# Attention and gated feed-forward on one core: the second batch's attention moved from the prologue into chunk 0's first layer

## The chip, the cores and the metric

The kernel runs on one core of a Trainium2 chip. A core has five engines with a queue of instructions each: TensorE (PE, matrix products), VectorE (DVE), ScalarE (ACT), GpSimd (POOL) and SyncE (SP, which here only issues transfers). Every queue is worked off in order; where an instruction needs another engine's result, it waits on a semaphore, and everything behind it in its queue waits too. The metric is the device time of one execution in microseconds (us); lower is better. The median of three runs before the change is 1016.38 us.

## What is computed

```python
# q, k, v: (8, 8, 576, 64) float32     w_gate, w_val: (512, 1536) float64     w_out: (1536, 512) float64
kv  = einsum('bhsd,bhse->bhde', k, v)          # one 64 x 64 matrix per batch and head
out = einsum('bhsd,bhde->bhse', q, kv)
x   = out / sqrt(mean(out * out, -1) + 1e-6) * g_norm
x   = x.transpose(0, 2, 1, 3).reshape(4608, 512)
y   = (sigmoid(x @ w_gate) * (x @ w_val)) @ w_out
```

The weights arrive as 64-bit floating point numbers, and the kernel turns them into float32 itself.

## The kernel before

**Tiling.** The 4608 tokens are nine chunks of 512. A batch has 576 tokens, so chunk 0 lies wholly in batch 0, and chunk 1 holds the last 64 tokens of batch 0 and the first 448 of batch 1. The hidden width 1536 is twelve blocks of 128. Chunk 0 goes through the feed-forward plainly: the first layer is twelve blocks of 8 matmuls of 128x512 (`Plain.mm`, L561: four over the contraction for the gate, four for the value), the second layer 48 matmuls (`second`, L808). Chunks 1 to 8 use a scheme with fewer products in each layer (26 sets of products, L932 and L1036), for which sums of blocks of weights (`w1_sums`, L741, on GpSimd), of x (`x_sums`, L830, on VectorE) and of hidden values (L722, mostly on GpSimd) are formed beforehand.

**Weights.** `convert(u)` turns one unit, 128x1024 numbers, from float64 into float32 in five VectorE steps and two ScalarE steps: `s0` takes the high bits of the mantissa (L179) and `s1` the exponent (L190); `a0` (L184) and `a1` (L195) are ScalarE's conversions of these two; `s2` (L200) adds the low word, `s3` (L204) the sign, `s4` (L211, L213) multiplies mantissa and exponent word. The exponent words lie in `cz`, a tile with two buffers in SBUF. There are 18 units: 0 to 11 serve the twelve first-layer blocks in their order, 12 to 17 the second layer, two blocks of rows each. A unit's 1 MB comes through `load_unit`, into three staging buffers.

**Attention, in two forms.** Batches 0 and 1 are handled early, by pairs of heads, eight pairs in all (`NE = 2 * NHP`). For a pair `attention(n)` has k-v products (KV, L276), their copy (KVO), the turn of q by TensorE (Q, L287) and its copy (QO), the product with q (U, L306), its square (SQ, ScalarE), sums (SUM, VectorE), root (ROOT, ScalarE), the norm (NORM, VectorE: reciprocal and one product), the turn of x (X, L333) and its copies (XO). Batches 2 to 7 are handled later in the other form, `feed(b)`: `load_late` brings k and v into `h_more`, `kv_mm` does all four pairs' k-v products at once (L366, L372), twelve ScalarE copies put them into `kvq` (L377), VectorE turns q in blocks of 32 (`turn`, L383), and `two_pairs` does U for two pairs (L407, 72 small matmuls into the tile `at` in PSUM, of which there is one), square, two sums, root, two norm operations on VectorE (L425) and the turns of x (L432), whose result 16 transfers on SP put into place. These steps stand at numbered places between the products of the chunk before.

**Order.** The prologue is written out by hand in `order`, a string of tokens: the steps above with the pair's number, `c0.1` and `a0.1` for conversion steps of a unit, `b0.1.2` for matmul 2 of the value half of first-layer block 0, `w2` for loading unit 2, and `warmN` for N matmuls without use. It interleaves eight pairs with blocks 0 to 3 of chunk 0 and units 0 to 4. As the root and the sigmoid need different tables of ScalarE, the first two blocks' results are copied out (CG, CV) and get their sigmoid (S) and product (M) once all eight pairs are through. From block 4 on `plain` runs: beside the first six matmuls of a block one conversion step each is placed, and the gate and the product of the block before at matmuls 0 and 2. Batch 2's `kv_mm` stands after block 8, its copies after block 9, the weight sums `w1_sums(0)` after block 10.

**Stores.** Rows of batches 0 and 1 leave the kernel in up to 96-row pieces, those of later batches in 32-row pieces, because the two forms of attention order tokens differently inside a batch (`store`, L503).

## Time and profile before

| | us |
|---|---|
| median of three runs (1016.28 to 1017.71) | 1016.38 |
| the profiled execution | 1015.84 |
| its span, first to last instruction | 1014.1 |
| TensorE busy | 1006.5 (99%) |
| VectorE busy | 727.1 (72%) |
| GpSimd busy | 598.9 (59%) |
| ScalarE busy | 350.2 (35%) |

The granted TensorE clock is full in the whole span. Between 100 and 160 us VectorE is busy for 8 to 10 of every 10 us and GpSimd for nearly all of them; between 160 and 260 us GpSimd is busy for 93 us. From 360 us on TensorE is busy without a break.

In the lines of the timeline the columns are: start (us from the span's start), length (us, of the whole merged group), engine, line, operation, output and inputs, shape, count, and in brackets the idle time before it and what ended it. An fp32 matmul has two records. Instructions overlap at their ends, so the distance from start to start is what one costs in a full queue.

### The profile page before, as it was taken

What the parts mean: (1) busy time and instruction counts of PE and PEld (TensorE: products, weight loads), DVE (VectorE), ACT (ScalarE), POOL (GpSimd) and SP (SyncE); (2) the same over time, 40 slices, a digit from 0 to 9 for tenths busy, and PEclk for the clock granted to TensorE, in tenths of its full rate; (3) what the DMA queues carried; (4) which work ended last, traced back from release to release, by engine and by line L of the source; (5) the groups of instructions that cost most, each with busy time, mean ns of one, the idle gap of its engine ahead of it and who ended that gap; (6) DMA issues with size and microseconds to landing.
All of it is one profiled execution on the core that took longest, in us unless ns stands there. A gap on an engine that the chain in (4) does not pass through costs nothing.

```text
span 1014.1 us, 18347 instructions
## 1 busy us (share of the span) xinstructions
PE 1006.5 (99%) x6914; PEld 828.0 (82%) x6914; DVE 727.1 (72%) x1211; ACT 350.2 (35%) x609; POOL 598.9 (59%) x965
## 2 busy tenths in 40 slices
PE   9999999999999999999999999999999999999998
PEld 8644447888888888888888888888888888888887
DVE  4899899899668846775678666866688556755672
ACT  4654422442154304441254115421453033213320
POOL 0001999998448642967177706962496439744963
PEclk9999999999999999999999999999999999999999
DMA  9975314644778468646765577556764546444514
GB/s 264 278 237 191 125 42 157 220 143 163 235 245 301 165 194 262 225 159 200 232 234 194 150 229 248 195 160 190 235 214 153 178 155 208 161 156 158 211 59 124
DMA packets 101128, 193.89 MB, mean 191 GB/s; under 512 B 27408, under 2 KB 74128, under 8 KB 101040
## 3 DMA queue, kind: packets, MB, share of 16 engines
q0 software_dynamic: 20976, 112.87, 32.9%
q1 hardware_dynamic: 72896, 77.75, 25.2%
q10 hardware_dynamic: 7168, 2.10, 0.9%
q8 instruction: 55, 0.90, 0.4%
q14 instruction: 33, 0.27, 0.1%
HBM read 160.04 MB, written 25.56 MB: 183 GB/s over the span
## 4 chain that ended last, share of the span: by engine, by line
PE 74%; POOL 2%; issue 0%; DVE 0%; POOLq 0%
PE mm L932 47%; PE mm L1036 24%; PE at L407 2%; PE at L366 1%; POOL h L722 1%; POOL w_ring L1007 0%; POOL h_more L722 0%; PE at L372 0%; POOL w L770 0%; DVE sg L902 0%; POOL w L1007 0%; POOLq L1007 0%
## 5 line engine op out<-in xcount | busy, mean ns | idle before, releaser
L932 PE MATMUL mm<-xs,w 128*128 128x256 f32 x1428 | 332.0, 380 | 0.0
L932 PEld LDWEIGHTS mm<-xs,w 128*128 128x128 f32 x1428 | 270.4, 190 | 37.4 <-DVE temps L902 0.3
L932 PE MATMUL mm<-xT,w 128*128 128x256 f32 x948 | 230.0, 380 | 0.0
L932 PEld LDWEIGHTS mm<-xT,w 128*128 128x128 f32 x948 | 179.4, 190 | 25.5 <-issue 1.0
L902 DVE TENSOR_TENSOR sg<-sg,mm 128x512 f32<-128x512 f32 (+1 forms) x176 | 100.8, 599 | 93.1 <-PE mm L932 45.7
L770 POOL DMA_DIRECT2D w<-kept x84 | 46.9, 558 | 190.7 <-PE mm L932 188.4
L1036 PE MATMUL mm<-w,h 128*128 128x256 f32 x630 | 143.4, 379 | 0.9 <-POOL h L894 0.5
L1036 PEld LDWEIGHTS mm<-w,h 128*128 128x128 f32 x630 | 119.5, 190 | 17.9 <-POOL h L894 0.9
L898 ACT COPY temps<-mm 128x512 f32<-128x512 f32 (+1 forms) x128 | 66.0, 537 | 190.0 <-PE mm L932 94.9
L894 POOL TENSOR_TENSOR h<-h,sg 128x512 f32<-128x512 f32 x72 | 97.6, 1372 | 50.3 <-DVE h L902 33.2
L722 POOL TENSOR_TENSOR h<-h 128x128 f32<-128x128 f32 x216 | 113.4, 537 | 16.5 <-DVE h_more L722 13.1
L1036 PE MATMUL mm<-w,h_more 128*128 128x256 f32 x474 | 108.2, 379 | 0.0
L891 ACT ACTIVATE sg<-sg 128x512 f32<-128x512 f32 x96 | 59.7, 630 | 131.4 <-DVE sg L902 131.4
L1036 PEld LDWEIGHTS mm<-w,h_more 128*128 128x128 f32 x474 | 90.1, 190 | 12.2
L898 ACT COPY sg<-mm 128x512 f32<-128x512 f32 (+1 forms) x112 | 57.1, 510 | 91.2 <-PE mm L1036 48.8
L722 POOL TENSOR_TENSOR h_more<-h 128x128 f32<-128x128 f32 x120 | 58.5, 490 | 33.9 <-DVE h L894 29.6
L561 PE MATMUL mm<-xT,w 128*128 128x512 f32 x176 | 77.7, 594 | 0.0
L902 DVE TENSOR_TENSOR temps<-temps,mm 128x512 f32<-128x512 f32 (+1 forms) x96 | 59.2, 617 | 25.5 <-PE mm L1036 17.2
L902 DVE TENSOR_TENSOR temps<-mm,temps 128x512 f32<-128x512 f32 (+1 forms) x64 | 39.8, 621 | 50.6 <-PE mm L1036 23.6
L898 ACT COPY h<-mm 128x512 f32<-128x512 f32 x48 | 28.1, 585 | 125.5 <-PE mm L932 110.5
L902 DVE TENSOR_TENSOR sg<-mm,sg 128x512 f32<-128x512 f32 (+1 forms) x64 | 39.6, 618 | 43.7 <-PE mm L932 21.9
L741 POOL TENSOR_TENSOR h_more<-w 128x256 f32<-128x256 f32 x10 | 12.8, 1299 | 97.4 <-PE at L366 97.4
(132 smaller groups left out, 1324.5 us busy)
## 6 DMA issues: line engine op xcount, KB each, us to landing
w<-kept POOLq DMA_DIRECT2D x42, 896.0 KB, 5.0
w<-kept POOLq DMA_DIRECT2D x90, 384.0 KB, 4.6
w<-kept POOLq DMA_DIRECT2D x42, 768.0 KB, 5.4
q<-in_q_dram SPq DMA_DIRECT2D x24, 288.0 KB, 3.0
out_dram<-sg SPq DMA_DIRECT2D x104, 64.0 KB, 1.7
st<-in_moe_w_gate_dram SPq DMA_DIRECT2D x12, 512.0 KB, 5.5
st<-in_moe_w_val_dram SPq DMA_DIRECT2D x12, 512.0 KB, 6.6
h_more<-in_k_dram SPq DMA_DIRECT2D x24, 256.0 KB, 5.0
```

The lines of the kernel that those rows point to most:

```text
L366: nc.tensor.matmul(ps[HD * e:HD * e + HD, n // 2, n % 2], mains[n, "k"][:, c], mains[n, "v"][:, c], start=(n % 2 == 0 and j == 0), stop=Fa ...
L407: nc.tensor.matmul(u[HD * e:HD * e + HD, r, o:o + HD], qTs[QB * r:QB * r + QB, (n0 + which) % 2, c:c + PH], kvq[QB * r:QB * r + QB, (n0 + ...
L561: nc.tensor.matmul(self.ps[i], w[("wg", "wv")[i], self.f][:, m, :], xT[self.c][:, m, :], start=(m == 0), stop=(m == NMT - 1), skip_group_c ...
L722: ops.append((eng, lambda v=v, x=x, sign=sign, y=y, eng=eng: eng.tensor_tensor(out=h_form(v, j), in0=h_form(x, j), in1=h_form(y, j), op=op ...
L741: nc.gpsimd.tensor_tensor(out=w1_slot(j, w_at[v]), in0=w1_slot(j, w_at[x]), in1=w1_slot(j, w_at[y]), op=op_of(sign))
L770: nc.gpsimd.dma_start(out=granule(g)[:, 0:n], in_=kept1[g // NPA % N3, g % NPA][:, 0:n])
L891: nc.scalar.activation(out=o["o" + step[1]], in_=o["o" + step[1]], func=AF.Sigmoid)
L894: mult.tensor_tensor(out=o[x], in0=o[x], in1=o[y], op=ALU.mult)
L898: nc.scalar.copy(out=o[out_], in_=o[expr])
L902: tt(out=o[out_], in0=o[x], in1=o[y], op=ALU.add if sign == "+" else ALU.subtract)
L932: nc.tensor.matmul(regions[name][1][:, g], ws[:, g], xf[c][wv], start=(new and g == 0), stop=True, skip_group_check=True)
L1036: nc.tensor.matmul(regions[name][1], h_form(hv, j), ws[:, j], start=(used[i] and j == 0), stop=(j == N3 - 1), skip_group_check=True)
```

## The change

Only batch 0's four pairs stay early (`NE = NHP`). The hand-written order ends with block 0 of chunk 0 and unit 1; CG, CV, S and M are gone, and the first block's sigmoid is read from PSUM as for the others. Blocks 1 to 11 go through `plain`, whose steps now come from a written table: place p is matmul p of these 88, and the names are `CV` (the next conversion step), `LL` and `LL2` (loads of k and v of batches 1 and 2), `KV`, `C0` to `C3` and `KV2`, `D0` to `D3` (k-v products and copies for the two batches), `Q0` to `Q3` (q loads), `t10` (turn of pair 1, half 0), `W0` (`w1_sums(0)`), and `a..`, `b..` for the steps of the two groups of two pairs. Batch 1 so takes the form of `feed`, with three differences: its q goes into parts of the hidden tiles `h_main`, which are not in use yet, its four rest loads are issued by SP, not by ScalarE, and its norm is 18 ScalarE activations with a scale for each partition. The exponent words of units 15, 16 and 17 lie in the tile `at` in PSUM. Rows of batch 1 are stored in 32-row pieces. From chunk 1 on the order of work is as before.

```diff
-    NE = 2 * NHP
+    NE = NHP
...
+            if b == 1:
+                i = n - NE
+                t = h_main[2 - i // 2].rearrange("p s c -> p (s c)")[0:NP, (i % 2) * 2 * NJ * HD:(i % 2 + 1) * 2 * NJ * HD]
+                t = t.rearrange("p (h c) -> p h c", h=2)
...
-                nc.scalar.dma_start(out=rest[...], in_=src[...])
+                (nc.sync if b == 1 else nc.scalar).dma_start(out=rest[...], in_=src[...])
...
-            d["p"] = p = by_block(raw.tile([P, UW], U32, tag="cz", name="cz", bufs=2))
+            if u < 15:
+                t = raw.tile([P, UW], U32, tag="cz", name="cz", bufs=2)
+            else:
+                t = at_ps()[:, 0:2].rearrange("p r c -> p (r c)").bitcast(U32)
+            d["p"] = p = by_block(t)
...
-    to_convert = deque((u, i) for u in range(5, len(units)) for i in range(5))
+    to_convert = deque((u, i) for u in range(2, len(units)) for i in range(5))
...
+            def norm(r):
+                for n in range(NJ):
+                    nc.scalar.activation(out=by_head(sq)[:, r, n], in_=by_head(d["u"])[:, r, n], func=AF.Copy,
+                                         scale=ms[:, r, n:n + 1])
+
+            if b == 1:
+                norms = [lambda: nc.vector.reciprocal(ms, ms)] + [lambda r=r: norm(r) for r in range(NQ)]
+            else:
+                norms = [lambda: u_norm(0), lambda: u_norm(1)]
...
-            if b < 2:
+            if b < NE // NHP:
...
-    def plain(c, u, ps):
+    def plain(c, u, ps, steps_at):
...
-            if at < 6:
-                convert_step()
+            for step in steps_at.get(at, ()):
+                step()
...
+    order = """w1 warm9 KV0 Q0 KVO0 QO0 U0 warm8 SQ0 SUM0 ROOT0 KV1 Q1 KVO1 NORM0 warm5 X0 QO1 U1 SQ1 XO0 c0.0 SUM1
+        ROOT1 c0.1 warm14 NORM1 KV2 warm2 Q2 a0.0 c0.2 KVO2 a0.1 c0.3 c0.4 QO2 X1 warm2 U2 SQ2 KV3 Q3 b0.0.0 KVO3 SUM2
+        w2 w3 XO1 QO3 U3 ROOT2 NORM2 c1.1 SQ3 a1.1 X2 b0.0.1 SUM3 c1.0 ROOT3 XO2 b0.1.0 b0.1.1 NORM3 X3 b0.1.2 a1.0
+        c1.3 c1.2 b0.0.2 c1.4 w4 XO3 b0.0.3 b0.1.3"""
...
+    places = """
+        1:CV,CV 2:CV,Q1 4:CV,CV 5:CV,CV 6:CV,LL,Q0 7:CV,CV 10:CV,CV 11:Q2 13:Q3 15:CV 16:CV,CV 17:t10
+        18:CV,CV 19:t00,t01 20:KV 21:t11 22:CV,CV,C1 23:CV,C0,C2,C3 25:CV 26:CV,CV 29:au,t20,t21,LL2 30:CV
+        31:t30,asq 32:CV,as0 33:t31 34:CV,as1,art 35:CV 36:arc,an0 37:an1 38:CV,an2 40:CV,CV 41:CV,ax0 43:ax1
+        44:bu 46:CV,bsq 48:CV,CV,bs0 50:CV 52:CV,CV 54:bs1 55:CV,CV,brt 57:CV,CV 58:CV 60:CV,brc 62:bn0,bn1
+        63:bn2 64:CV 65:CV,CV,CV 66:CV,CV 67:CV 68:KV2,D2 69:D3 70:D0,D1 71:bx0 72:CV 73:W0 75:bx1
+        80:CV,CV,CV,CV,CV 84:CV 87:CV,CV
+    """
...
+        plain(0, f, ps, {at: at_place.get(2 * NMT * (f - 1) + at, ()) for at in range(2 * NMT)})
```

## The prediction

> **What bounds the kernel now.** I read the page's busy shares first (TensorE 99%), then the ten-microsecond windows, then the chain of waits, then each engine's timeline up to 265 us, because the diff touches nothing later. TensorE's queue first:

> ```profile
> 22.48 1.93 PE L561 MATMUL mm<-xT,w 128*128 128x512 f32 x4
> ...
> 53.25 44.80 PE L561 MATMUL mm<-xT,w 128*128 128x512 f32 x104
> 97.98 2.09 PE L366 MATMUL at<-h_more 128*64 128x64 f32 x64
> ...
> 100.38 14.00 PE L561 MATMUL mm<-xT,w 128*128 128x512 f32 x32
> 114.22 7.03 PE L561 MATMUL at<-xT,w 128*128 128x512 f32 x16
> 121.09 41.36 PE L808 MATMUL mm<-w,h 128*128 128x512 f32 x96
> 162.29 1.03 PE L932 MATMUL mm<-xT,w 128*128 128x256 f32 x4
> ```

> No idle time stands beside any of these lines: from 22.5 us (first real matmul of chunk 0) to 162.3 us (chunk 1 begins) TensorE runs through. Each fp32 matmul has two records, so 104 records in 44.80 us are 52 matmuls of 0.86 us. What is removed from this queue is worth its full length, as long as VectorE and GpSimd keep up. VectorE's load is the next view: two weight units, without GpSimd beside it and with it.

> ```profile
> 68.25 0.69 DVE L179 TENSOR_SCALAR w<-st 128x1024 uint32<-128x1024 uint32 x1
> 68.86 0.69 DVE L190 TENSOR_SCALAR cz<-st 128x1024 uint32<-128x1024 uint32 x1
> 70.16 1.22 DVE L200 SCALAR_TENSOR_TENSOR w<-st,w 128x1024 f32<-128x1024 uint32 x1 [0.62 <-ACT w L184]
> 71.30 0.68 DVE L569 TENSOR_TENSOR h<-mm,sg 128x512 f32<-128x512 f32 x1
> 71.90 1.21 DVE L204 SCALAR_TENSOR_TENSOR cz<-st,cz 128x1024 uint32<-128x1024 uint32 x1
> 73.15 1.28 DVE L211 SCALAR_TENSOR_TENSOR w<-w,g_col,cz 128x1024 f32<-128x1024 f32 x1
> ...
> 137.57 1.21 DVE L179 TENSOR_SCALAR w<-st 128x1024 uint32<-128x1024 uint32 x1
> 138.70 1.22 DVE L190 TENSOR_SCALAR cz<-st 128x1024 uint32<-128x1024 uint32 x1
> 140.00 1.60 DVE L200 SCALAR_TENSOR_TENSOR w<-st,w 128x1024 f32<-128x1024 uint32 x1
> 141.51 1.75 DVE L204 SCALAR_TENSOR_TENSOR cz<-st,cz 128x1024 uint32<-128x1024 uint32 x1
> 143.30 1.63 DVE L213 TENSOR_TENSOR w<-w,cz 128x1024 f32<-128x1024 f32 x1
> ```

> By start to start a unit costs 4.85 us alone, 0.6 more with a gate's product, 0.62 more when the second step waits for ScalarE; with GpSimd busy it costs 7.3. A block of 8 matmuls takes TensorE 6.89. The last unit ends at 152.2 us and TensorE needs it at 121.09 + 40 x 0.862 = 155.5, a slack of 3.3. Last, what holds chunk 1:

> ```profile
> 182.76 1.27 POOL L894 TENSOR_TENSOR h<-h,sg 128x512 f32<-128x512 f32 x1
> 185.70 6.22 POOL L894 TENSOR_TENSOR h<-h,sg 128x512 f32<-128x512 f32 x3 [1.67 <-DVE h L902]
> ```

> GpSimd works without a gap from 98.7 us (weight sums) to 184.0, waits 1.67 us for VectorE, and then runs almost without a gap to 260 us, where the chain of waits passes from it to TensorE for the rest of the kernel. Its start at 185.7 hangs on chunk 1's products, so an earlier chunk 1 moves it, provided that the weight sums are done by then.

> [...]0.69 becomes 1.21, 1.21 becomes 1.75, 1.28 becomes 1.63. [...]with the exponent words in PSUM, L190 keeps about 1.2 us, and L204 and L213[...] should fall back to 1.2. No run here shows them there.[...]

> **The change, part by part.** *Prologue.* Four of the eight early pairs go. Each costs TensorE by start to start 0.85 (L276) + 0.55 (L287) + 0.74 (L306) + 0.55 (L333) = 2.7 us, in all 10.8. Added are one more k-v pass (97.98 to 100.38, 2.40) and two of the 144-record products of L407 (184.83 to 186.61 and 211.10 to 212.83: 1.78 and 1.73), in all 5.9. Two warm-up counts change, which fill waits only. In the queue 4.9 us are gained; before it also lost about 0.7 in small issue gaps between its pieces (139.8 us from 22.48 to 162.29, less 124.0 for 144 matmuls and 15.1 for attention), most of which goes too: 5.5.

> Given back first: block 0 loses its cover. In the new order it needs pairs 2 and 3, and around it stand only U3, X2, X3 (1.85 us). The chain after Q3 (22.0, as before) is U3 at 23.4, square 0.70, sum 0.8, root 0.30, norm 1.05, transposes 0.6, copies 0.76, with a first and a second conversion step of unit 1 in VectorE's and ScalarE's queues between: X3 near 28.0, its copy out at 29.4. TensorE has about 0.9 us to wait in all and ends block 0 at 32.0; unit 1 is converted at 31.5. Then 11 blocks.

> *VectorE.* It must convert units 2 to 17 from 31.5 on: 10 x 4.85 + about 1.2 for the one that meets GpSimd + three at 6.7 + three at about 6.4 (PSUM) = 89; 12 gate products 7.2; eight turns (L383, 0.52) 4.2; four sums (L416, 0.7) 2.8; reciprocals 0.4; eight turns of x (L432, 0.38) 3.0: 106.6 us. Walked down in the order of the new queues, it waits in addition for ScalarE: 0.62 at five units, 1.15 for TensorE to be halfway through the first L407 group, 1.5 for the root (two table loads in ScalarE's queue), 1.4 and 1.0 for the norm of 18 activations and the sigmoid behind it, 1.3 behind the second set of twelve kvq copies (4.47 us), about 10.5 with small ones. The last unit is ready at 148.4. On the way (ready / needed, us): unit 2 36.9 / 38.9, unit 4 48.4 / 55.1, unit 8 84.3 / 87.4, unit 11 104.4 / 110.5, unit 12 113.7 / 117.4, unit 14 129.0 / 131.2, unit 17 148.4 / 151.8. The least slack is 2 us, so conversions stop nothing, but there is not more than that. If PSUM brings no relief, three units cost 0.9 more each and the last slack is 0.7.

> *ScalarE.* The norm moves from two VectorE operations of 0.75 per two pairs to 18 x 0.24 = 4.3 us of ScalarE. Behind it are queued the next table load and the sigmoid, hence the waits above. The `at` tile is single: the second L407 group at place 44 (74.1) must wait for the first norm's last read, 70.8 + 4.3 = 75.1. TensorE loses 1.0 there. The second k-v pass meets the second norm's end with nothing lost (97.7 against 97.5). The bounds for an activation are the trace's 0.20 start to start (the 0.76 us of three copies of 576 elements, less 0.86 ns per element) and 0.36 (the 32x256 copies): the wait is 0.3 to 3.2 us. I take 0.24.

> *Transfers.* The eight k, v loads and four rest loads of batch 1 now stand on SP behind unit 5's load, which waits for unit 2's L204 at 35.7. 1.05 MB + 2.4 MB at the 275 GB/s or so that the first 50 us show in the windows are drained at about 48.5; the k-v pass comes at 49.2 and reads the rest last, at 51. The cover is 1 to 2 us. SP also gets q loads and 16 transfers of x (0.6 us of issue each) between weight loads; those loads land 5 us or more ahead of use. Stores of batch 1 rows become 32-row pieces: same bytes, more issues, no one waits.

> *GpSimd.* Its start moves from 98.74 to about 98.5. Beside conversions it did 40 sums in 54 us, afterwards 36 in 30 us. [...]I estimate 42 sums by 148.4 and the end at 177 instead of 182.8; with no relief 181.8. VectorE's h then comes at about 182.3, so GpSimd is on time either way, within 1 us.

> **Sum.** 5.5 - 0.9 (block 0) - 1.0 (L407) - 0.2 (small waits) = 3.4 us, all of it handed down the chunk 1 chain. Against the profiled execution, 1015.84 us (span 1014.1 and 1.7 around it): 1012.4. The median, 1016.38, stands 0.5 above the profiled one, so 1013.0.

> **Rivals.** *Slower: VectorE becomes the bound of the first 150 us.* Place: the conversion queue. It decides once VectorE runs more than 2.2 us later than my walk; beyond 5.6 the gain is gone. For it: the trace has a 3.41 us stop (a gate behind twelve copies) and six of 0.62, and the new queue has more crossings with ScalarE. If the other ten units also wait 0.62 (6.2) and a 3.4 stop comes once more: 9.6 late, less 2.2, TensorE 7.4 later than forecast; 1020.4, and about 1018 if half of the 0.62 waits occur. Against it: 106.6 us of work in a window of 120. *No change: the cover of a transfer[...] fails.* If k, v land 3 us late, or GpSimd's sums end near 185[...], the 3.4 are eaten: 1015 to 1017. Against it: bandwidth in the trace is even, and GpSimd has the 1.67 us. *All waits vanish:* no wait for the norm and none in block 0: 1011.

> **How the numbers follow.** Forecast with its smaller variants, 1011 to 1014.3: 0.58. No change: 0.17. Slower by VectorE: 0.25. What this kernel's measurement can tell from no change is 0.2%, 2 us. The range takes 1011.0 at the lower end and reaches into the slower case up to 1018.0; the likeliest case's own range is 1011.0 to 1014.3. Faster 0.58, same 0.17, slower 0.25.

> **What would show it.** Right: chunk 1's first L932 at about 159 us in TensorE's timeline (162.29 before), block 1 from about 32, one wait of about a microsecond at the second L407 group, L204 and L213 of the last three units near 1.2 us, GpSimd's L894 group of three near 182. Wrong: idle time of TensorE released by VectorE's w (L211 or L213 before), by a k, v transfer, or by GpSimd in chunk 1 beyond the present 1.6 us.

## The result and the profile after

The kernel after takes 1020.28 us (median of six runs, 1018.36 to 1023.73) against 1016.22 before: 1.0040 times as long, 95% interval 1.0025 to 1.0055. So it is slower by 4 us, and its median lies 7.3 us above the forecast. The profiled execution took 1019.73 us, with a span of 1018.0.

TensorE's queue first, as the timeline of the kernel after has it. The lines answer to those shown of before (L561 is now L581, L366 is L372, L407 is L416, L808 is L813, L932 is L937).

```profile
23.98 1.05 PE L581 MATMUL mm<-xT,w 128*128 128x512 f32 x2
...
30.46 21.62 PE L581 MATMUL mm<-xT,w 128*128 128x512 f32 x50
52.02 2.09 PE L372 MATMUL at<-h_more 128*64 128x64 f32 x64
...
62.34 1.91 PE L416 MATMUL at<-kvq,qTs 32*64 32x64 f32 x144
64.19 13.14 PE L581 MATMUL mm<-xT,w 128*128 128x512 f32 x30
77.26 1.80 PE L416 MATMUL at<-kvq,qTs 32*64 32x64 f32 x140
82.06 0.48 PE L416 MATMUL at<-kvq,qTs 32*64 32x64 f32 x4 [3.00 <-issue]
82.47 23.63 PE L581 MATMUL mm<-xT,w 128*128 128x512 f32 x48
106.03 2.08 PE L372 MATMUL at<-h_more 128*64 128x64 f32 x64
...
124.85 41.36 PE L813 MATMUL mm<-w,h 128*128 128x512 f32 x96
166.05 1.03 PE L937 MATMUL mm<-xT,w 128*128 128x256 f32 x4
```

Chunk 1 begins at 166.05 us, where it began at 162.29 before and where I had put it near 159. From there on both kernels run alike. Two lines stand out. The second L416 group (place 44) breaks off after 140 of its 144 records, and the last four come 3.00 us later, released by "issue", which means that the profile shows nothing the engine waited for. And the 48 records behind it take 23.6 us, where 24 matmuls of 0.861 us are 20.7. The window view says why; its columns are the stretch, its length, busy time of PE, PEld, DVE, ACT and POOL (with instructions), PEclk, the share of DMA time and GB/s.

```profile
77.00:78.00 1.00, 1.00 (x68) 0.74 (x70) 0.59 (x2) 0.98 (x2) 0.00 (x0) 1.00 1.04 353
78.00:79.00 1.00, 1.00 (x95) 0.92 (x81) 0.00 (x0) 0.99 (x3) 0.00 (x0) 1.00 1.08 372
79.00:80.00 1.00, 0.06 (x5) 0.00 (x0) 0.98 (x2) 1.00 (x1) 0.00 (x0) 1.00 0.84 229
80.00:81.00 1.00, 0.00 (x0) 0.00 (x0) 1.00 (x4) 0.02 (x1) 0.00 (x0) 1.00 0.37 88
81.00:82.00 1.00, 0.00 (x0) 0.00 (x0) 1.00 (x2) 0.93 (x1) 0.00 (x0) 0.62 0.35 86
82.00:84.00 2.00, 1.94 (x6) 1.12 (x6) 1.59 (x3) 1.58 (x3) 0.00 (x0) 0.50 0.45 112
84.00:86.00 2.00, 2.00 (x3) 0.67 (x2) 0.56 (x1) 0.26 (x1) 0.00 (x0) 0.50 0.56 134
86.00:88.00 2.00, 2.00 (x4) 0.92 (x3) 0.00 (x0) 0.00 (x0) 0.00 (x0) 0.50 1.09 380
88.00:90.00 2.00, 2.00 (x5) 0.85 (x5) 1.93 (x3) 0.00 (x0) 0.00 (x0) 0.98 0.16 49
```

The granted clock is halved from 81.2 to 88.1 us (0.62 in the window from 81 means that it fell 0.24 us into it). So the kernel loses 3.5 us in and around the stop (82.47 - 77.26 = 5.21, where a group takes 1.75) and 2.9 us to the half clock.

What was TensorE short of? The view of the DMA queues has a row of the kind "instruction", with packets, MB and its share of the same 16 engines:

```profile
q8 instruction: 55, 0.90, 0.4%
```

55 packets and 0.90 MB make 16 KB each. I take them for TensorE's instructions: no other engine has more than 1,300 counted instructions, TensorE has 14,000. The numbers fit: by the begin of packet 2, 469 of TensorE's records have started, by that of packet 55 14,010, which is 255.5 records to a packet; I count with 256. And in the whole trace only one wait of TensorE is released by "issue", the 3.00 us here. Counting TensorE's records (matmuls and weight loads, four to an fp32 matmul, 288 to a L416 group, and a few instructions that only wait) up to the begin of each packet gives this for the kernel after:

```
packet   begins   took   records started by then   of these not yet made up by packets
  4       57.78   1.15          1078                          310
  5       65.08   0.95          1391                          367
  6       79.42   1.22          1729                          449
  7       91.00   1.00          1767                          231
  8      109.55   0.94          2008                          216
```

Packet 6 begins 2.16 us after the group's start. By then TensorE has stood for 0.36 us: 281 records of the group have started, and the next one, number 1729, does not come. It comes at 82.06, 1.4 us after the packet has landed (80.64). At the other 54 packets of this kernel the last column lies between 148 and 418.

The rest of the profile looks as forecast. VectorE's last unit, with the exponent words in PSUM:

```profile
147.30 0.88 DVE L184 TENSOR_SCALAR w<-st 128x1024 uint32<-128x1024 uint32 x1
148.10 1.24 DVE L199 TENSOR_SCALAR at<-st 128x1024 uint32<-128x1024 uint32 x1
149.40 1.26 DVE L209 SCALAR_TENSOR_TENSOR w<-st,w 128x1024 f32<-128x1024 uint32 x1
150.58 1.22 DVE L213 SCALAR_TENSOR_TENSOR at<-st,at 128x1024 uint32<-128x1024 uint32 x1
151.83 1.22 DVE L222 TENSOR_TENSOR w<-w,at 128x1024 f32<-128x1024 f32 x1
```

1.22 us each for the steps that were 1.75 and 1.63, and the unit is ready at 153.05, where TensorE needs it at 124.85 + 34.4 = 159.3. GpSimd's sums end at 180.6, and it then waits 5.08 us for chunk 1; before, its first product of h (182.76) followed the sums without a wait:

```profile
179.86 0.72 POOL L731 TENSOR_TENSOR sg<-sg,w_ring 128x256 f32<-128x256 f32 x1
185.66 1.28 POOL L899 TENSOR_TENSOR h<-h,sg 128x512 f32<-128x512 f32 x1 [5.08 <-ACT sg L896]
189.47 6.22 POOL L899 TENSOR_TENSOR h<-h,sg 128x512 f32<-128x512 f32 x3 [2.53 <-DVE h L907]
```

### The profile page after: what moved, and what is told of

It is laid out like the page before. It is cut to its first block, busy times and chain, and to the rows that moved or that the text cites. A ratio compares the mean times of both kernels' runs of the same rounds, so it can differ in the third digit from the quotient of the medians.

```text
span 1018.0 us, 18558 instructions
## 1 busy us (share of the span) xinstructions
PE 1005.8 (99%) x6988; PEld 825.9 (81%) x6988; DVE 723.8 (71%) x1215; ACT 360.5 (35%) x639; POOL 589.6 (58%) x965
## 4 chain that ended last, share of the span: by engine, by line
PE 74%; POOL 2%; issue 0%; DVE 0%; POOLq 0%
PE mm L937 47%; PE mm L1041 24%; PE at L416 2%; PE at L372 1%; POOL h L712 1%; POOL w_ring L1012 0%; POOL h_more L712 0%; PE at L378 0%; POOL w L760 0%; DVE sg L907 0%; POOL w L1012 0%; POOLq L1012 0%
## 5 line engine op out<-in xcount | busy, mean ns | idle before, releaser
L937 PE MATMUL mm<-xs,w 128*128 128x256 f32 x1428 | 332.0, 380 | 0.0
L937 PEld LDWEIGHTS mm<-xs,w 128*128 128x128 f32 x1428 | 270.4, 190 | 37.4 <-DVE temps L907 0.4
L937 PE MATMUL mm<-xT,w 128*128 128x256 f32 x948 | 230.0, 380 | 0.0
L937 PEld LDWEIGHTS mm<-xT,w 128*128 128x128 f32 x948 | 179.4, 190 | 25.5 <-issue 1.0
L899 POOL TENSOR_TENSOR h<-h,sg 128x512 f32<-128x512 f32 x72 | 97.7, 1374 | 56.4 <-DVE h L907 34.0
L581 PE MATMUL mm<-xT,w 128*128 128x512 f32 x176 | 79.9, 612 | 0.0
L712 POOL TENSOR_TENSOR h_more<-h 128x128 f32<-128x128 f32 x120 | 58.7, 493 | 33.7 <-DVE h L899 29.4
L907 DVE TENSOR_TENSOR temps<-mm,temps 128x512 f32<-128x512 f32 (+1 forms) x64 | 39.8, 622 | 51.2 <-PE mm L1041 23.6
L731 POOL TENSOR_TENSOR h_more<-w 128x256 f32<-128x256 f32 x10 | 9.5, 967 | 105.5 <-DVE cz L213 105.5
```

The lines of the kernel that those rows point to most:

```text
L581: nc.tensor.matmul(self.ps[i], w[("wg", "wv")[i], self.f][:, m, :], xT[self.c][:, m, :], start=(m == 0), stop=(m == NMT - 1), skip_group_c ...
L712: ops.append((eng, lambda v=v, x=x, sign=sign, y=y, eng=eng: eng.tensor_tensor(out=h_form(v, j), in0=h_form(x, j), in1=h_form(y, j), op=op ...
L731: nc.gpsimd.tensor_tensor(out=w1_slot(j, w_at[v]), in0=w1_slot(j, w_at[x]), in1=w1_slot(j, w_at[y]), op=op_of(sign))
L899: mult.tensor_tensor(out=o[x], in0=o[x], in1=o[y], op=ALU.mult)
L907: tt(out=o[out_], in0=o[x], in1=o[y], op=ALU.add if sign == "+" else ALU.subtract)
L937: nc.tensor.matmul(regions[name][1][:, g], ws[:, g], xf[c][wv], start=(new and g == 0), stop=True, skip_group_check=True)
```

## The experiments

All numbers of TensorE's queue are put together in the table at the end of this section; times are medians, and the kernel before had 1016.1 to 1016.4 beside them.

**First question: is the packet late because data stands in front of it in the DMA engines?** In the kernel after they are full from 76.5 to 79.5 us. Three runs move work away from that stretch or out of it.

*e1: batch 2's k and v load later.*

```diff
-        ... 29:au,t20,t21,LL2 30:CV
+        ... 29:au,t20,t21 30:CV
-        44:bu 46:CV,bsq 48:CV,CV,bs0
+        44:bu 46:CV,bsq 47:LL2 48:CV,CV,bs0
```

> The load of batch 2's k and v (LL2, 2.1 MB with its rests) moves from place 29 to place 47, behind the second group of L416; nothing else is changed. Theory A (TensorE's instructions are fetched through the same DMA engines; at 79.8 us one fetch came late because data transfers were queued in front of it[...]): the stop of 3.0 us inside the group and the half clock from 81.6 to 88.4 us vanish, chunk 1's first L937 stands near 160 us instead of 166.05, the time is 1012 to 1014.5. Theory B (the burst of short matmuls outruns the fetch whatever the transfers do): the stop stays at 2.5 to 3.5 us at the same place, the half clock too, 1018 to 1021. Theory C (what I forecast as the slower case, VectorE late with the conversions): no change in the place of chunk 1, 1018 to 1021, with TensorE's waits released by VectorE.

*e2: the second group four places later.*

```diff
-        44:bu 46:CV,bsq 48:CV,CV,bs0 50:CV 52:CV,CV 54:bs1
+        46:CV 48:CV,bu,CV 50:CV,bsq 52:CV,CV,bs0 54:bs1
```

> The second L416 group moves from place 44 to place 48 (some 3.5 us later), its square and first sum with it, the transfers stay where they are, so that the group begins behind the backlog of transfers (the DMA share falls to 0.37 at 80 us). Theory A (a fetch of instructions queued behind data): the stop inside the group falls below 1 us, no half clock, chunk 1's first L937 near 160 us, 1012 to 1014.5. Theory B (the burst alone): again about 3 us of stop, now near 81 to 84 us, and half clock after it, 1018 to 1021.

*e3: the transfers of x later.*

```diff
-        ... 41:CV,ax0 43:ax1
-        44:bu 46:CV,bsq 48:CV,CV,bs0 50:CV 52:CV,CV
+        ... 41:CV
+        44:bu 46:CV,ax0 47:ax1 48:CV,CV,bsq 50:CV 51:bs0 52:CV,CV
```

> The two turns of x of the first two pairs (ax0, ax1) with their 16 transfers move from places 41 and 43 to 46 and 47, behind the second L416 group; bsq and bs0 move by two or three places, LL2 stays. If the 16 transfers of x (small pieces, 77.6 to 83.6 us) are what the late fetch of instructions is queued behind: the stop and the half clock vanish, 1012 to 1014.5. If it is the 2.1 MB of LL2 with the weight unit behind it: the stop stays between 2 and 3 us, 1017 to 1021. If the burst alone does it: stop of 3 us, 1018 to 1021.

e1 took 1020.09 and e3 1020.41, like the kernel after; e2 took 1014.76. The timeline of e1 at the group:

```profile
77.68 1.83 PE L416 MATMUL at<-kvq,qTs 32*64 32x64 f32 x140
82.57 0.48 PE L416 MATMUL at<-kvq,qTs 32*64 32x64 f32 x4 [3.06 <-issue]
```

So neither LL2 nor the transfers of x are what the packet waits for, and my theory fell in the form in which I had put it. That e2 loses the stop agreed with it (its time lies 0.3 us above the range that I had set), but e2 changes more than the transfers beside the group: it also moves it by 16 records in the count modulo 256, and behind the end of the norm.

**Second question: is it the group's place in the count of instructions?** In all runs that stopped, the group begins at record 1448 of the trace, that is at 168 modulo 256. (Counted with four instructions each, the 377 matmuls and transposes ahead of the group make 1508, with 27 more that only wait. The trace has 87 fewer, because it shows two records and not four for a transpose; whether the program has four, no record shows. The table keeps to the trace's count.) Warm-up matmuls without use, in the prologue 60 us earlier, shift that count by four records each, and all times by 0.24 us each.

*f1, f2, f3, f4*: the number of warm-ups in the prologue (f3 on top of e2, the others on top of the kernel after).

```diff
 f1   -... ROOT1 c0.1 warm14 NORM1 ...   +... ROOT1 c0.1 warm18 NORM1 ...
 f2   -... ROOT1 c0.1 warm14 NORM1 ...   +... ROOT1 c0.1 warm7 NORM1 ...
 f3   -... ROOT1 c0.1 warm14 NORM1 ...   +... ROOT1 c0.1 warm10 NORM1 ...
 f4   -U0 warm8 SQ0 ... warm14 NORM1     +U0 warm4 SQ0 ... warm3 NORM1
```

> Four warm-up matmuls are added to the kernel after (warm14 becomes warm18 in the prologue); they are 16 more records in TensorE's queue ahead of everything that follows, and 0.94 us of work without use. Theory D (phase: TensorE's instructions come in packets of 256, each asked for when the count of records passes a fixed point modulo 256, near 168; the next ones arrive 4 to 5 us after that[...]; a group of L416 has 288 in 1.8 us, so it runs dry only when it begins within some 20 records of that point, as it does at record 1448 = 168 + 5 x 256 in the kernel after): the second L416 group begins at 184 modulo 256, as it did in the run with that group four places later, the stop of 3.0 us and the half clock vanish, chunk 1's first L937 near 160.5 us, 1014 to 1015.5: faster by 5 to 6 us through more work. Theory B (the burst outruns the fetch wherever it stands; it was the later place that helped): the stop stays, 1020.5 to 1022.

> Seven warm-up matmuls are taken out of the kernel after (warm14 becomes warm7): 28 records and 1.65 us less ahead of KV2. Theory D (phase): the second L416 group begins at 140 modulo 256 and does not stop near 76 us, but later groups of L416, of batches 3 and 5 and so on, move to 164 and 171 (189 and 215 us before the shift) and to 168 and 155 (517 and 542 us), so stops of 1 to 3 us appear there, which no run has had there so far. Block 0 begins 1 to 1.6 us earlier, because pair 2's k-v products no longer stand behind useless matmuls. Time 1012 where those stops cost nothing, up to 1025 where each costs 3 us and half clock behind it. Theory B (the burst outruns the fetch wherever it stands): stop at 76 us stays, none later, 1018.5 to 1020. If pair 2 has to wait for its data anyway (the warm-ups only fill a wait, as I forecast): block 0 begins at 24 us as before.

> The kernel with the second L416 group at place 48, now with four warm-up matmuls fewer (warm14 becomes warm10): 16 records and 0.94 us of useless work less. Theory D (phase): the group is back at 168 modulo 256, so it stops again for about 3 us, near 84 us, with half clock behind it; some later groups come to 166, 175 and 179 and may stop too: 1019 to 1030, slower than the same kernel with 0.94 us more work (1014.76). Theory B' (it was the later place, with its light transfers, that helped): no stop, 1013 to 1014.5.

> Fifteen warm-up matmuls are taken out of the kernel after (warm8 becomes warm4, warm14 becomes warm3): 60 records, so that by theory D (phase) the second L416 group begins at 108 modulo 256 and no later group comes nearer to 168 than 139 or 191: no stop anywhere. If the useless matmuls had cost their length (up to 3.5 us): block 0 begins 1.5 to 2.5 us earlier, chunk 1's first L937 at 157 to 158.5, 1010.5 to 1012.5. If they fill waits for k, v, the norms and unit 0, as I forecast: TensorE idles 2 to 3 us before KV2, block 0 begins where it did, 1013 to 1014.5, and where the granted clock falls in that idle time, later still (1015 to 1017).

f1 agrees: with four useless matmuls more, the kernel takes 1015.15 us instead of 1020.28. Its timeline has the group whole, and no half clock follows it:

```profile
78.47 1.83 PE L416 MATMUL at<-kvq,qTs 32*64 32x64 f32 x144
80.22 20.87 PE L581 MATMUL mm<-xT,w 128*128 128x512 f32 x48
...
161.04 1.03 PE L937 MATMUL mm<-xT,w 128*128 128x256 f32 x4
```

f2 (1018.05) goes the other way as expected: nearly no stop at its second group (0.31 us behind it), but stops in two later groups, at 171 and 168 modulo 256, where no run had one; the groups that came to 164 and 155 did not stop, against what I had set for them. Here is the first of the two:

```profile
207.61 1.75 PE L416 MATMUL at<-kvq,qTs 32*64 32x64 f32 x139
211.10 0.33 PE L416 MATMUL at<-kvq,qTs 32*64 32x64 f32 x5 [1.74 <-issue]
```

f4 (1012.55) has no stop anywhere. f3 missed: its group is back at 168, but it stopped for 0.55 us only, and the run took 1014.29 instead of 1019 or more. The count alone is not the whole cause.

```profile
85.59 0.33 PE L416 MATMUL at<-kvq,qTs 32*64 32x64 f32 x4 [0.55 <-issue]
```

That the count is a part of it, all traces together show. After 40 us the timelines of the fifteen kernels have sixteen waits of TensorE released by "issue", of 0.21 to 3.06 us: in L416 groups, once shortly behind one, and three times at other products (f1 has one of 0.61 us at 301.5). Every one of them comes at record 193 or 194 modulo 256, so to within one record they stand whole multiples of 256 apart. And in the eight runs of the table that have one in the group or shortly behind it, TensorE goes on 2.4 to 2.9 us after packet 6 begins (82.06 after 79.42 in the kernel after, 85.59 after 82.69 in f3).

**Third question: what else is needed?** In the four runs with a stop of about 3 us (after, e1, e3, e4) the packet begins within 0.3 us of the end of the stretch in which the DMA engines are full, also in e1 and e3. What is left in that stretch there is the 1 MB of weight unit 10, issued at 74.9 us in the kernel after. *g1* moves this load alone; TensorE's queue stays the same to the instruction.

```diff
-            if u > 1:
+            if u > 1 and u != 7:
                 load_unit(u + NST)
...
-        44:bu 46:CV,bsq 48:CV,CV,bs0
+        44:bu 46:CV,bsq 47:L10 48:CV,CV,bs0          # L10: load_unit(10)
```

> The kernel after, with one load moved: the 1 MB of weight unit 10 is issued at place 47, behind the second L416 group, instead of 2.4 us ahead of it; TensorE's queue is the same to the instruction. In all runs so far the late fetch of TensorE's instructions began within half a microsecond of the end of a stretch in which the DMA engines were full (76.5 to 79.5 us in the kernel after), also where LL2 or the transfers of x had been moved away, so what is left in that stretch is this unit. Theory E (phase and a fetch queued behind the unit's load, both needed): the fetch begins at 77 to 78 us instead of 79.8, the stop falls from 3.0 us to below 1, no half clock, 1013.5 to 1015.5. Theory D alone (phase; the fetch takes its 4 to 5 us whatever is in front of it): stop 3.0 us, 1019.5 to 1021.

g1 took 1017.17 us, between the two theories. Two windows show that the DMA engines stand nearly still; a third, of 0.2 us, holds the packet (82 GB/s in 0.2 us are its 16 KB). The timeline follows:

```profile
77.00:78.00 1.00, 1.00 (x60) 0.66 (x65) 0.67 (x2) 0.98 (x2) 0.00 (x0) 1.00 0.01 3
78.00:79.00 1.00, 1.00 (x103) 0.98 (x90) 0.00 (x0) 0.99 (x3) 0.00 (x0) 1.00 0.08 16
...
78.20:78.40 0.20, 0.20 (x40) 0.20 (x31) 0.00 (x0) 0.20 (x1) 0.00 (x0) 1.00 0.40 82
```

```profile
77.34 1.79 PE L416 MATMUL at<-kvq,qTs 32*64 32x64 f32 x140
80.86 0.33 PE L416 MATMUL at<-kvq,qTs 32*64 32x64 f32 x4 [1.74 <-issue]
```

The packet now begins 0.92 us after the group's start (78.26) instead of 2.16, the stop is 1.74 instead of 3.00, and the half clock lasts 3.4 us instead of 6.8. So the load in front of the packet made up 1.3 us of the stop; the other 1.74 come with empty DMA engines.

In f3 the packet begins 0.6 us *before* the group. f3 lacks two things. Unit 10's load, issued at 77.48 there, has gone through: the DMA engines are full from 79.5 to 82.0 us, and the packet begins at 82.69. And the group has no wait for the norm: ScalarE's last activation of it (L457) ends 3.6 us ahead of the group in e2 and f3, but only 0.18 us ahead of it in the kernel after and in g1 (77.08 and 77.26; 77.16 and 77.34). *h1* takes that wait out of g1: the group one place later, one warm-up fewer, so that it begins at the same instruction.

```diff
-... ROOT1 c0.1 warm14 NORM1 ...
+... ROOT1 c0.1 warm13 NORM1 ...
-        44:bu 46:CV,bsq 47:L10
+        45:bu 46:CV,bsq 47:L10
```

> The run with unit 10's load behind the second L416 group (1017.17; stop of 1.74 us), with that group one place later (45 instead of 44, so 0.86 us later, after the norm's last read of the tile at) and one warm-up matmul fewer (warm14 becomes warm13), so that the group begins at the very same instruction of TensorE's queue (1508 matmul instructions ahead of it in both). Theory G (the next packet is asked for [...]only when the norm is through): without the wait the fetch begins before or with the group, not 1.2 us after its start, and the stop falls from 1.74 to below 0.6 us, without half clock; 1013.5 to 1015.5. Theory D alone (the instruction's number decides): fetch 1.2 us after the group's start, stop 1.5 to 2 us, half clock, 1016 to 1018.

The group in h1, then the window that holds the packet, and the norm's activations in g1 and in h1:

```profile
77.51 1.76 PE L416 MATMUL at<-kvq,qTs 32*64 32x64 f32 x140
79.97 0.33 PE L416 MATMUL at<-kvq,qTs 32*64 32x64 f32 x4 [0.70 <-issue]
...
77.40:77.60 0.20, 0.20 (x7) 0.09 (x12) 0.00 (x0) 0.20 (x1) 0.00 (x0) 1.00 0.30 82
...
73.39 3.77 ACT L457 ACTIVATE sqs<-at,ms 128x64 f32<-128x64 f32 x18
72.64 3.78 ACT L457 ACTIVATE sqs<-at,ms 128x64 f32<-128x64 f32 x18
```

1014.99 us, in the range of theory G. The packet begins with the group (77.54 against 77.51), as theory G had it; the stop of 0.70 is a little above what I had set. In both runs the packet begins 1.1 us after the end of the norm's last activation (77.16 and 78.26 in g1, 76.42 and 77.54 in h1), so it moves with the norm and not with the group. The norm's late end is thus a third part of the stop, of about 1 us. For the profiled executions of these three runs, 3.00 = 1.26 of the load, 1.04 of the norm and 0.70 of the group and the count alone. By what way the norm holds the packet back, no record shows. (In h1's profiled execution, 1021.35 us, a later batch's k-v products waited 3.8 us for v.)

**Does the half clock belong to the stop, or to any idle time?** *g2* makes TensorE wait with its instructions at hand, on top of f4: one useless matmul ahead of block 8, whose operand GpSimd makes by five products without use.

```diff
+        if u == 8:
+            nc.tensor.matmul(ps[0][:, 0:P], spare_sg[:, 0:P], ident, start=True, stop=True, ...)
...
+        for _ in range(5):
+            nc.gpsimd.tensor_tensor(out=spare_sg, in0=spare_sg, in1=spare_sg, op=ALU.mult)
```

> On top of the run with fifteen warm-up matmuls fewer (1012.55), TensorE is made to wait once in chunk 0 with its instructions at hand: before block 8 (near 88 us) stands one matmul without use that needs a tile which GpSimd fills by five products of 128x512 (added work without use, begun when block 6's hidden values are there). By 1.27 us for one such product the wait is 2.5 to 3.5 us. Theory F (any idle time of TensorE of this length is followed by half clock for 3.4 or 6.8 us, as after the stops at L416): the granted clock falls to 0.5 behind it, the whole costs the wait and 1.7 to 3.4 us more, 1016.5 to 1019. Rival (half clock belongs to the burst of short matmuls or to the missing instructions): full clock behind the wait, 1015 to 1016.

The wait came out longer than planned, as the row of the waits of TensorE and three windows show:

```profile
PE mm L598 <- POOL sg L782: 6.2, 1, 6.2
```

```profile
92.00:93.00 1.00, 0.00 (x0) 0.00 (x0) 0.96 (x2) 0.80 (x2) 0.95 (x1) 1.00 0.00 0
93.00:94.00 1.00, 0.00 (x0) 0.00 (x0) 1.00 (x2) 0.00 (x0) 0.97 (x1) 0.74 1.07 172
...
98.00:100.00 2.00, 2.00 (x4) 0.83 (x3) 1.96 (x3) 1.80 (x10) 0.00 (x0) 0.50 0.00 0
100.00:101.00 1.00, 1.00 (x4) 0.43 (x3) 1.00 (x2) 1.00 (x7) 0.00 (x0) 0.85 0.87 164
```

Half clock from 93.5 to 100.3 us, and 1021.25 us in all: 8.7 more than f4, for a wait of 6.2. So half clock follows idle time of TensorE with another cause, too. The wait was twice as long as planned, but waits nearer to 3 us stand in other traces: in h1's, 3.8 us in two parts for v, up to 292.9 us, with half clock from 291.6 to 298.5; in g2's own, 2.3 us for v at 15 us, with half clock from 18.4 to 21.8.

**Two parts of the change undone.** *e4* puts the exponent words of the last three units back into SBUF (on top of the kernel after), *g3* gives batch 1's norm back to VectorE (on top of f4).

```diff
 e4   -            if u < 15:                              +            if u < 18:
 g3   -  norms = [lambda: nc.vector.reciprocal(ms, ms)] + [lambda r=r: norm(r) for r in range(NQ)]
      +  norms = [lambda: u_norm(0), lambda: u_norm(1)] + [lambda: None for _ in range(NQ - 1)]
```

> Undoes one part: the exponent words of the last three units lie in SBUF again (u < 18), all else is as in the kernel after. By my sum the three units' L199, L213 and L222 cost 1.2, 1.75 and 1.63 us instead of 1.24 each, so 0.9 us more for a unit; the last unit is ready near 155.8 instead of 153.05, needed at 159.3, so TensorE does not wait; GpSimd's sums end about 5 us later, near 185.5 instead of 180.6, and chunk 1's L899 triple comes at 189.5 for the products of chunk 1: nothing lost. Theory[...]: 1019.5 to 1021.5, chunk 1 at 166. Rival (GpSimd becomes late): 1 to 3 us slower than the kernel after, with the triple later than 190.5.

> Undoes one part, on top of the run with fifteen warm-up matmuls fewer (1012.55): the norm of batch 1 is done by VectorE in two operations for two pairs as in the later batches, not by 18 activations of ScalarE. VectorE gets about 3 us more work between 65 and 98 us and loses the waits of 1.0 to 1.4 us behind the activations and the sigmoid; TensorE loses the wait of some 0.4 to 0.8 us at the second L416 group. By my sum VectorE had 2 us of slack at the tightest unit: within 1 us of 1012.55 either way. Rival (VectorE is so near the bound that 3 us more of it show): 1014 to 1015.5, with TensorE's waits released by VectorE's w.

e4 took 1021.49 (1019.55 to 1022.13; after 1018.36 to 1023.73). VectorE's two steps and GpSimd's end of the sums, from e4's timelines:

```profile
153.18 1.74 DVE L213 SCALAR_TENSOR_TENSOR cz<-st,cz 128x1024 uint32<-128x1024 uint32 x1
154.95 1.63 DVE L222 TENSOR_TENSOR w<-w,cz 128x1024 f32<-128x1024 f32 x1
```

```profile
187.25 0.73 POOL L731 TENSOR_TENSOR sg<-sg,w_ring 128x256 f32<-128x256 f32 x1
187.93 7.53 POOL L899 TENSOR_TENSOR h<-h,sg 128x512 f32<-128x512 f32 x4
```

By start to start the unit costs 7.28 us instead of 5.86, and the sums end at 188.0, 7.4 later than after, more than the 5 that I expected. It costs nothing there because chunk 1 is late: the group of h ends at 195.5, and at 195.7 in the kernel after. g3 took 1011.81 (ratio to before 0.9957, interval 0.9945 to 0.9968), f4 1012.55 (0.9954, 0.9938 to 0.9970): no difference, so no gain of the norm on ScalarE by itself can be told. The profiled execution of g3 (1017.05) shows something else: with the warm-ups gone, the third pair's k-v products waited 5.07 us for v.

**A better version.** *g4*, on top of f4, moves the copy KVO2 ahead of `c0.2`.

```diff
-... Q2 a0.0 c0.2 KVO2 a0.1 c0.3 ...
+... Q2 a0.0 KVO2 c0.2 a0.1 c0.3 ...
```

> On top of the run with fifteen warm-up matmuls fewer (1012.55), the copy KVO2 is placed ahead of unit 0's step c0.2 in VectorE's queue, where it stood behind it (L289 at 19.49 us, behind the 1.22 us of L209); the number of TensorE's instructions is unchanged, so the phase stays. TensorE's wait of 0.72 us before U2 should go, and the square and the sum behind it come 1.1 us earlier, unit 0 is ready 0.2 us later: chunk 1 0.4 to 1 us earlier, 1011.5 to 1012.2. Rival: block 0 then waits for unit 0 or for the norms of pairs 2 and 3 instead, and nothing is gained, 1012.3 to 1012.8.

1012.15 us, ratio 0.9962 (0.9948 to 0.9976): U2's wait is gone, and block 0 then waits 0.5 us for unit 0. In the profiled execution chunk 1 begins at 157.41 (158.57 in f4's), but with f4's ratio of 0.9954 no gain can be told. f4, g3 and g4 all beat the kernel before, by 3.8 to 4.6 us.

The columns of the table up to the last but one are from one profiled execution of each run; the half clock is that behind the group.

| run | group begins, us | at record, mod 256 | packet 6 begins | stop, us | half clock behind it, us | chunk 1 at | median |
|---|---|---|---|---|---|---|---|
| after | 77.26 | 168 | 79.42 | 3.00 | 6.8 | 166.05 | 1020.28 |
| e1 | 77.68 | 168 | 79.91 | 3.06 | 6.8 | 166.81 | 1020.09 |
| e3 | 77.28 | 168 | 79.27 | 2.85 | 6.8 | 165.84 | 1020.41 |
| e4 | 77.84 | 168 | 79.98 | 2.78 | 3.4 | 165.23 | 1021.49 |
| e2 | 82.90 | 184 | 81.58 | none | none | 162.07 | 1014.76 |
| f1 | 78.47 | 184 | 74.81 | none | none | 161.04 | 1015.15 |
| f2 | 75.65 | 140 | 79.63 | 0.31, behind it | none here | 158.80 | 1018.05 |
| f4 | 75.96 | 108 | 77.98 | none | none | 158.57 | 1012.55 |
| f3 | 83.28 | 168, load and norm through | 82.69 | 0.55 | none | 163.23 | 1014.29 |
| g1 | 77.34 | 168, load moved | 78.26 | 1.74 | 3.4 | 163.63 | 1017.17 |
| h1 | 77.51 | 168, load moved, norm through | 77.54 | 0.70 | none | 160.19 | 1014.99 |

## Why the prediction was wrong

The missing step. The sum "5.5 - 0.9 (block 0) - 1.0 (L407) - 0.2 (small waits) = 3.4 us" has no term for the supply of TensorE's own instructions. I took the duration of a L407 group (1.78 us) from the profile of before and set it at a new place, as if it were a property of the group. But 288 records in 1.8 us are more than the 255.5 that a packet makes up, and at place 44 three things met: the group began at 168 modulo 256, so that it came to 193 of the next 256 before its end, 1 MB of a weight unit was in front of that packet, and the group's first instruction hung on the norm, which ended only 0.18 us ahead of it. By f1 the stop and the half clock behind it are worth 1020.28 - (1015.15 - 0.94) = 6.1 us, of the 7.3 by which I was off; most of the rest is the next two terms, 1.9 late at block 0 and 1.0 not lost at L407. None of my rivals had this mechanism: the slower case was to come from VectorE's conversions, and no idle time of TensorE in the kernel after is released by w.

The term of block 0. I wrote "Two warm-up counts change, which fill waits only" and ended block 0 at 32.0 us. It ended at 33.9. By the diff five of the six counts change (10, 3, 3, 13, 2, 6 become 9, 8, 5, 14, 2, 2). A warm-up costs 0.236 us, and the fourteen ahead of KV2 hold it until 18.73, where it began at 16.46 before. f4, with fifteen fewer, has KV2 at 15.96 and block 1 at 32.6; from f1 to f4, nineteen fewer are worth 2.6 us of the 4.5 that they last. They do fill a wait where v comes late: in g3's profiled execution, without them, KV2 waited 5.07 us.

The term of L407. TensorE was to lose 1.0 at the second group, waiting for the norm. The 18 activations took 3.78 us (0.21 each, where I had taken 0.24, between the 0.20 and 0.36 of the trace of before), and ended at 77.08. The group's weight loads stand idle for 0.8 us there, but so they do in e2 and f3, where the norm is long through, and the matmuls ahead of them still run: as a wait it costs TensorE nothing. What it did cost is the third part of the stop. (The table load behind the norm, at 77.10, takes 1.28, and the next activation begins at 78.39.)

What was right. The queue: from block 1 to chunk 1 f4 needs 126.0 us, by my numbers 126.9 (158.9 - 32.0) with the 1.0 of L407 in it. Without the stop and with the warm-ups cut, chunk 1 begins at 158.57 and the time is 1012.55; the forecast had 159 and 1013.0. That the two are so near is in part luck: block 1 begins 0.6 late, and the 1.0 of L407 is not lost. VectorE: no conversion stopped TensorE, in after or in f4, so the slower rival is refuted in its place. (Its milder number was also mis-summed: half of the 0.62 waits make 3.1 + 3.4 - 2.2 = 4.3, so 1017.3 and not about 1018.) The transfers of k and v came in time. PSUM: 1.22 to 1.24 us for the steps in question (L199, L213, L222), where I had expected about 1.2 without a run that showed it; GpSimd's sums end at 175.9 in f4 (forecast 177) and its group of three begins at 181.99 ("near 182"). And e4's 7.4 us of delay show what the relief is for: put against f4, by my estimate it would end the sums near 183.3, behind the 178.6 at which GpSimd's first product of chunk 1 begins. No run undid it there.

What stays open: in e2 and f1 the group stands at the same instruction count, yet in f1 the packet begins 3.66 us ahead of the group, with 15 records left to it, and in e2 1.32 us, with 3. In f1 that is before unit 10's load is issued (74.81 and 76.17); in e2 the load is issued at 77.09, the DMA engines are full from 79 to 81.5, and the packet begins as they come free. That fits the load in front of the packet, but no run moves the load alone there. It also means that f1 took the packet out from behind the load as well as shifting the count; what the load is worth is seen from g1, not from f1.

## What to carry to other kernels

Here TensorE stopped after some 280 records of a group of 288 that takes 1.8 us elsewhere. Where your kernel has such a stretch, look at when the next 16 KB packet comes before you trust the duration that the same stretch had elsewhere. The sign in the profile was idle time released by "issue" in the middle of one group, at the same count modulo 256 (193 or 194); with full DMA engines in front of the packet it was longer (3.00 against 1.74 us), but it came without them, too. Two remedies worked here: to shift the count (a few instructions more or fewer ahead of it, which can bring other groups to the bad count, as f2 did), and to keep large loads and late waits away from its start. To split it with longer work was not tried. Price idle time of TensorE above its length: the stops of 1.46 us and more, and the wait of 6.2, had half clock behind them, for 3.4 or 6.8 us.

## What the runs showed of the hardware that I had not expected

The half clock lasted 6.8 us behind the stops of 2.85 to 3.06 (after, e1, e3) and the wait of 6.2 (g2), 3.4 us behind stops of 1.46, 1.74 and 2.78 (f2, g1, e4); behind 0.70 or 0.55 (h1, f3) there was none. What decides between the two lengths, no run shows: a stop of 2.78 had 3.4, one of 2.85 had 6.8.
